# Loads of k and v moved ahead, stores and a small product moved back, in a fused attention and double expert-layer kernel

## The chip, the cores and the metric

The kernel runs on one core of one Trainium2 chip. The time is the device time of that core in microseconds (us). Before the change the median of three runs is 1707.53 us (1704.66 to 1713.23).

The engines are named as the profile names them: PE is TensorE's matrix multiply and PEld its weight load, DVE is VectorE, ACT is ScalarE, POOL is GpSimd, and SP is the engine that issues most transfers. A transfer is issued by SP or POOL and carried by 16 DMA engines.

## The reference

All inputs are float64 in memory; the kernel reads them as pairs of 32-bit words and converts them.

```python
# attention: B=8, H=8, S=576, D=64; k and v are averaged over 8 neighbours
k_p = k.reshape(B, H, 72, 8, D).mean(axis=3)
v_p = v.reshape(B, H, 72, 8, D).mean(axis=3)
scores = (1/sqrt(D)) * q @ k_p.T
attn = exp(scores - max) ; attn = attn / (sum(attn) + 1e-9)
x = attn @ v_p                                 # 4608 tokens x 512
# first layer: d_ff 1024
x = (((x @ w1) * (x @ w2)) @ w3) @ w_out
# second layer: d_ff 1536
xn = x / sqrt(mean(x*x) + 1e-6) * rms_g
g = xn @ w_gate
out = (g * sigmoid(g) * (xn @ w_val)) @ w_out2
```

## The kernel before, in words

The 4608 tokens are cut into nine blocks of 512 (`NB`, index `i`); the attention has eight batches of 576 tokens (index `b`). Products are made in three passes of a split operand (`mm3`, lines 93 to 95: high by high, high by low, low by high), so one product of a 128-column weight slice with a block is 4 x 3 = 12 matmuls.

The stages, in the order of the code:

- **Opening** (lines 543 to 590). `w3 @ w_out` is multiplied out once (`wps`, line 573), its split halves go to DRAM (`wpd`, lines 587 and 588, issued by POOL), and the attention of batch 0 and the first four pairs of products of block 0 are woven in.
- **Blocks 0 to 8** (lines 798 to 842). `ab(i, m, s)` makes `x @ w1` (s = 0) or `x @ w2` (s = 1) for one of eight slices `m`; for s = 1 DVE multiplies the two into `hh` or `hl` (line 540) and SP stores that to `hd` (line 541). There are 16 such products in a block. `positions(i)` says behind which of the 16 the steps of the next batch's attention stand: `S` the scores (line 299) with maximum and exponential, `N` the division (line 327), `T` the transposes, which are DVE's from batch 2 on (line 342), `av_steps` the product with v (line 404) and its split into `xh` and `xl` (lines 411 and 412), `kT` and `Q` the transposes of k and q (lines 262 and 281).
- **k and v** come in through `pool_four`: SP loads half of the eight neighbours into a tile `kv` (line 223), POOL issues a second, adding transfer of the other half once the first has landed (line 224), and `pool_sum` on DVE adds the rest (line 228) into `kp` or `vp` (line 231). Each of k and v is two tiles. The tile is one of three buffers of the pool `raw_p`.
- **The weights of the second layer** are converted in the background (`gv_steps`, 12 groups, one step behind each product by the `prep` ticker): a raw load of float64 words (line 111) into `raw_p`, the conversion (`s1`, `s2`), sums of quarters (line 725), a split into `wst` and two stores to `wd` (line 738, POOL).
- **The y stage** (lines 1193 to 1212): `second` multiplies h by the folded weights, eight products of 12 matmuls for a block. `y_end(i)` squares and stores the result (`f` tiles from a pool of five), and hands back three steps, of which one is taken behind each product of the following block: `sq_split`, nothing, and `rms`, whose two matmuls (lines 673 and 674) sum the squares.
- **The second layer** (lines 1216 on): `gv` for block 0, then `quad` for pairs of blocks.

The order in which each engine and queue runs its instructions is fixed when the program is built, by the framework's scheduler with its own estimate of times. It keeps to the order of the code only roughly: it brings an instruction forward when by its estimate the engine is idle and the operands are there. Buffers of a pool are given out in the order of the code. So `wC_p` (four buffers, `w`) holds first the folded weights `wph` and `wpl` of two groups, then `wf` and two `wst` of each background group.

Of the kernel before, what the change touches and what calls it, by code (L numbers as in the profile page):

```python
# [11 lines left out]
I32 = mybir.dt.int32  # L12
# [9 lines left out]
def kernel(  # L22
# [17 lines left out]
    nc = tc.nc  # L40
    B, H, S, D = q.shape
    P = 128
# [39 lines left out]
    def hxtile(nm):  # L82
        return hx_p.tile([P, 512], F32R, tag=nm, name=nm)

    def wtile(pool, nm):
        return pool.tile([P, 4, 512], F32R, tag="w", name=nm)
# [11 lines left out]
    class Conv:  # L98
# [5 lines left out]
        def s0(self):  # L104
            pool, tag, bufs = self.pool if isinstance(self.pool, tuple) else (self.pool, "raw", None)
            self.raw = pool.tile([P, 1024], I32, tag=tag, name="raw", bufs=bufs)
            src = self.src.bitcast(I32)
            dst = self.raw
            if len(src.shape) == 3:
                dst = dst.rearrange("p (i c) -> p i c", i=src.shape[1])  # L110
            nc.sync.dma_start(out=dst, in_=src)
# [371 lines left out]

    def load_cols(n, srcs, his, los):
        c, r = divmod(n, 2 * KD)
        s, kk = divmod(r, KD)
        return Conv(
            srcs[s][kk * P : (kk + 1) * P, c * 512 : (c + 1) * 512],
            raw_p,
            then=lambda f: split(his[s][c][:, kk, :], los[s][c][:, kk, :], f),  # L490
        )

    def load_w12(n):
        return load_cols(n, (w1, w2), (w1h, w2h), (w1l, w2l))

# [33 lines left out]

    a0 = {}  # L530

    def ab(i, m, s):
        wh, wl = ((w1h, w1l), (w2h, w2l))[s]
        ps = mm_feat(wh, wl, *xtile(i), m)
        if s == 0:
            a0[i, m] = ftile()
            nc.scalar.copy(a0[i, m], ps)
        else:
            hf = hxtile("hh" if m % 2 else "hl").bitcast(F32)
            nc.vector.tensor_tensor(out=hf, in0=ps, in1=a0.pop((i, m)), op=ALU.mult)  # L540
            nc.sync.dma_start(out=hdram[i][m], in_=hf)

# [98 lines left out]
    def ybank(i):  # L641
        if i % 2:
            return psum()
        return py_p.tile([P, 512], F32, tag="y", name="y")

    def y_end(i):
# [24 lines left out]
        def rms():  # L671
            ps = ybank(i)
            nc.tensor.matmul(ps[:1], ones, sp[0], start=True, stop=False)
            nc.tensor.matmul(ps[:1], ones, sp[1], start=False, stop=True)
            row = ftile()
            nc.scalar.copy(row[:1], ps[:1])
            nc.sync.dma_start(out=sdram[i : i + 1], in_=row[:1])
            ss = const.tile([P, 4], F32, tag="ss", name="ss", bufs=2)
            nc.sync.dma_start(out=ss, in_=sdram[i].rearrange("(p c) -> p c", p=P))
            nc.vector.tensor_scalar(  # L680
                out=ss, in0=ss, scalar1=1.0 / DM, scalar2=1e-6, op0=ALU.mult, op1=ALU.add
            )
            nc.gpsimd.tensor_tensor(out=ss, in0=ss, in1=mhalf, op=ALU.pow)
            nc.sync.dma_start(out=rdram[i].rearrange("(p c) -> p c", p=P), in_=ss)

        return [sq_split, lambda: None, rms]

# [13 lines left out]
    def gv_steps(G, s, kp):  # L701
# [30 lines left out]
        def put(j):  # L732
            f = cell["f"]
            c = 2 * G + j
            st = ptile("wst").rearrange("p (f l c) -> p f l c", f=8, l=2)
            split(st[:, :, 0, :], st[:, :, 1, :], f[:, j])
            for z in range(2):
                nc.gpsimd.dma_start(
                    out=wdram[s, c, z][:, :, kp],
                    in_=st[:, 4 * z : 4 * z + 4].bitcast(F32),  # L740
                )
            ready.add((s, c, kp))

        cs = []
        for z in range(2):
            k0 = (2 * z + kp) * P
            src = w[k0 : k0 + P, G * 512 : (G + 1) * 512]
            cs.append(Conv(src, raw_p, out=lambda z=z: quart(z), view=view))
            cs[z].on_act = True
# [6 lines left out]
            lambda: put(0),  # L756
            lambda: put(1),
        ]
# [9 lines left out]
    def positions(i):  # L768
# [7 lines left out]
        ]  # L776
        pos[2] = [lambda: A.N(0), A.load_v]
        for t in range(1, NTL):
# [7 lines left out]
            ]  # L786
        pos[8] += [A.v]
        pos[12] += [lambda: A.T(NTL - 1, 0), lambda: A.T(NTL - 1, 1)]
        pos[13] += av_steps(b, i + 1)
        if b + 1 < B:  # L790
            C = atts[b + 1]
            pos[9] += [C.k0]
            pos[10] += [lambda: C.q(0)]
            pos[13] += [C.k1, lambda: C.q(1)]
            pos[15] += [C.kT, lambda: C.Q(0, 0), lambda: C.Q(0, 1)]
        return pos

    c1 = conv_steps([load_w12(n) for n in range(8, 16)], 2)
    preB.close()
# [4 lines left out]
    col_tiles(wA_p, W12, (w1h, w1l, w2h, w2l))  # L804
    att_py.append(1)
    cv = Ticker(c1, 1)
    cv.run(6)
# [15 lines left out]
    for i in range(1, NB):  # L823
# [6 lines left out]
        for n, (m, s) in enumerate((m, s) for m in range(KF1) for s in range(2)):  # L830
# [4 lines left out]
            if i == NB - 1 and n == 5:  # L835
                prep.flush()
                wph[:], wpl[:] = [], []
                for g in range(2):
                    for l, lst in enumerate((wph, wpl)):
                        lst.append(wtile(wC_p, "wp"))  # L840
                        nc.sync.dma_start(out=lst[g].bitcast(F32), in_=wpdram[g][l])
        xt.pop(i)

    def rtile(nm, dt=F32R):
# [376 lines left out]
    for c in range(NCH):  # L1221
# [9 lines left out]
        for f in range(2):  # L1231
# [4 lines left out]
            if c and f == 0:  # L1236
                o_mm(0, 2 * c - 1)
                tick()
        if c == 0:
            while todo:  # L1240
                todo.pop(0)()
        if c == 3:
# [68 lines left out]
```

## Time and profile before

| | |
|---|---|
| median of three runs | 1707.53 us |
| the profiled execution | 1718.17 us |
| its span, first to last instruction | 1716.4 us |
| PE busy | 1623.1 us, 95% of the span, 7250 matmuls |
| DVE busy | 1021.8 us, 60% |
| ACT busy | 658.3 us, 38% |
| POOL busy | 95.0 us, 6% |
| mean granted TensorE clock | 0.975 of full speed |
| bytes moved | 322.53 MB, mean 188 GB/s |

The busy shares are averages over stages with different limits. PE idles for some 93 us of the span (1716.4 less 1623.1), and a granted clock below 1 means that a part of its busy time ran at half speed. The rows below say where.

### The profile page before, as it was taken

How to read it: one execution, taken by the hardware profiler on the slowest of the kernel's cores; microseconds unless marked ns; L12 is line 12 of the kernel's file. 1: busy time of each engine (PE TensorE's matmuls, PEld its weight loads, DVE VectorE, ACT ScalarE, POOL GpSimd, SP SyncE). 2: the span in 40 equal slices, each digit the busy share in tenths (PEclk: the TensorE clock that was granted, in tenths of full speed). 3: DMA queues.
4: the chain of work that ended last, by engine and by line, in shares of the span. 5: the costliest groups of instructions: out<-in, count | busy, mean ns of one | idle time of the engine just before them, and what ended most of it. 6: DMA issues, size and time to landing. Idle time of an engine off the chain costs nothing.

```text
span 1716.4 us, 19990 instructions
## 1 busy us (share of the span) xinstructions
PE 1623.1 (95%) x7250; PEld 1296.5 (76%) x7250; DVE 1021.8 (60%) x1813; ACT 658.3 (38%) x1567; POOL 95.0 (6%) x107
## 2 busy tenths in 40 slices
PE   6797998798798999998999999999999999999999
PEld 3465777677586788886877888888888888888887
DVE  7675798696887842564574243567355744465344
ACT  3555544444444422453441133343333334234322
POOL 0001020111101010010010000000000000000000
PEclk9998999899898999998999999999999999999999
DMA  9948466556646465577456674457354745455531
GB/s 261 238 132 199 128 164 163 149 164 162 186 122 194 146 230 207 194 254 254 142 188 224 225 270 162 181 194 269 139 219 177 273 175 200 162 202 198 184 109 74
DMA packets 147461, 322.53 MB, mean 188 GB/s; under 512 B 52505, under 2 KB 79129, under 8 KB 129442
## 3 DMA queue, kind: packets, MB, share of 16 engines
q1 hardware_dynamic: 126210, 276.13, 47.7%
q0 software_dynamic: 21152, 45.12, 9.8%
q8 instruction: 57, 0.93, 0.2%
q14 instruction: 42, 0.34, 0.1%
HBM read 247.75 MB, written 73.44 MB: 187 GB/s over the span
## 4 chain that ended last, share of the span: by engine, by line
PE 68%; DMA 11%; DVE 11%; issue 7%; ACT 2%; POOL 1%; SPq 0%; POOLq 0%; ACTq 0%; DVEq 0%
PE ps L93 14%; PE ps L94 14%; PE ps L95 14%; PE o L95 5%; PE o L94 5%; PE o L93 5%; DMA kv<-in_v_dram 5%; DVE aT L342 3%; PE y L93 2%; PE y L94 2%; PE y L95 2%; DMA raw<-in_moe_w_dram 2%; PE pa L299 2%; DMA raw<-in_moe_w_out_dram 1%; DMA ydram<-f 1%
## 5 line engine op out<-in xcount | busy, mean ns | idle before, releaser
L93 PE MATMUL ps<-xf,wr 128*128 128x512 f32 x576 | 224.3, 389 | 0.0
L95 PE MATMUL ps<-xf,wr 128*128 128x512 f32 x576 | 224.1, 389 | 0.0
L94 PE MATMUL ps<-xf,wr 128*128 128x512 f32 x576 | 224.1, 389 | 0.0
L95 PE MATMUL o<-oh,hcl 128*128 128x512 f32 x384 | 149.6, 389 | 0.0
L94 PE MATMUL o<-ol,hch 128*128 128x512 f32 x384 | 149.4, 389 | 0.0
L93 PE MATMUL o<-oh,hch 128*128 128x512 f32 x384 | 149.4, 389 | 0.0
L1067 ACT COPY f<-ps 128x512 f32<-128x512 f32 x144 | 84.4, 586 | 163.8 <-PE ps L95 158.4
L342 DVE STREAM_TRANSPOSE aT<-s 32x256 f32<-32x256 f32 x324 | 140.8, 434 | 4.4
L93 PEld LDWEIGHTS ps<-xf,wr 128*128 128x128 f32 x576 | 108.1, 188 | 23.0 <-ACT f L1067 0.4
L95 PEld LDWEIGHTS ps<-xf,wr 128*128 128x128 f32 x576 | 108.1, 188 | 22.4
L94 PEld LDWEIGHTS ps<-xf,wr 128*128 128x128 f32 x576 | 108.1, 188 | 22.3
L93 PE MATMUL ps<-xh,w1h 128*128 128x512 f32 x288 | 123.2, 428 | 0.1
L1071 DVE TENSOR_TENSOR f<-y,f 128x512 f32<-128x512 f32 x48 | 33.2, 691 | 143.1 <-PE y L95 143.1
L314 ACT ACTIVATE s<-pa,mx 128x72 f32<-128x72 f32 (+1 forms) x280 | 85.2, 330 | 80.3 <-DVE mx L311 80.3
L94 PE MATMUL ps<-xl,w1h 128*128 128x512 f32 x288 | 115.6, 403 | 0.0
L95 PE MATMUL ps<-xh,w1l 128*128 128x512 f32 x288 | 114.9, 401 | 0.1
L93 PE MATMUL ps<-xh,w2h 128*128 128x512 f32 x288 | 112.5, 391 | 1.9 <-DVE hh L540 1.7
L95 PE MATMUL ps<-xh,w2l 128*128 128x512 f32 x288 | 113.1, 393 | 0.0
L94 PE MATMUL ps<-xl,w2h 128*128 128x512 f32 x288 | 112.8, 392 | 0.0
L127 ACT ACTIVATE raw<-raw 128x512 int32<-128x512 uint32 x76 | 51.8, 683 | 127.1 <-DMA raw<-in_moe_w_dram 35.4
L1153 DVE TENSOR_TENSOR acc<-o,acc 128x512 f32<-128x512 f32 x64 | 43.5, 689 | 75.5 <-PE o L95 75.0
L95 PEld LDWEIGHTS o<-oh,hcl 128*128 128x128 f32 x384 | 72.1, 188 | 15.4 <-DVE hcl L1093 0.6
(187 smaller groups left out, 3253.1 us busy)
## 6 DMA issues: line engine op xcount, KB each, us to landing
wr<-wd SPq DMA_DIRECT2D x96, 1024.0 KB
wd<-wst POOLq DMA_DIRECT2D x48, 512.0 KB, 5.9
hr<-hd SPq DMA_DIRECT2D x36, 512.0 KB
raw<-in_moe_w_dram SPq DMA_DIRECT2D x32, 512.0 KB
oh<-od SPq DMA_DIRECT2D x15, 1024.0 KB
ol<-od SPq DMA_DIRECT2D x15, 1024.0 KB
wr<-wd SPq DMA_DIRECT2D x24, 512.0 KB
raw<-in_moe_w_out_dram SPq DMA_DIRECT2D x20, 512.0 KB
```

The lines of the kernel that those rows point to most:

```text
L93: nc.tensor.matmul(o, lh, rh, start=first, stop=False, skip_group_check=part)
L94: nc.tensor.matmul(o, lh, rl, start=False, stop=False, skip_group_check=part)
L95: nc.tensor.matmul(o, ll, rh, start=False, stop=last, skip_group_check=part)
L127: nc.scalar.activation(self.low, low_u, AF.Copy, scale=2.0**-29)
L299: nc.tensor.matmul(ps[:n, (p % 2) * 2 * SP : (p % 2 + 1) * 2 * SP], qT_t[t // 2][:, t % 2, p, :n], kT[:, p, :], start=True, stop=True,)
L314: nc.scalar.activation(s_t[t][:n, h, :SP], pv[:, j, :], AF.Exp, bias=mx[:, j, :], accum_out=den_t[t][:n, h, :],)
L342: nc.vector.transpose(aT[32 * kb : 32 * kb + 32, :, s0 + 32 * i : s0 + 32 * i + 32], s_t[t][32 * i : 32 * i + 32, :, 32 * kb : 32 * kb + 32],)
L1067: nc.scalar.copy(t, bank)
L1071: nc.vector.tensor_tensor(out=t, in0=bank, in1=t, op=ALU.add)
L1153: nc.vector.tensor_tensor(out=a, in0=ys[j], in1=a, op=ALU.add)
```

## The change

- `k0` and `k1` (load and sum of k) stand behind products 6 and 12 of a block and no longer 9 and 13; the load of v stands behind product 13 of the block before and no longer behind product 2 of its own, and its sum behind product 4, no longer 8. For batch 1 the load of v stands before the last weights of the first layer.
- The raw tiles of the background weights (`gv_steps`) and of the last eight loads of w1 and w2 (`c1`) are halves of a `wC_p` buffer, `rawp`, and no longer from `raw_p`.
- The stores of `wst` and of h are issued a step, or a product, later.
- `rms` is taken six products after `y_end` and no longer three. For the last block its product takes a `psum()` bank, and the loop that emptied the list after the first chunk of the second layer is gone.

```diff
+    def raw_halves():
+        half = []
+
+        def get():
+            if not half:
+                t = wC_p.tile([P, 2048], I32, tag="w", name="rawp")
+                half.extend([t[:, :1024], t[:, 1024:]])
+            return half.pop(0)
+
+        return get
...
         def s0(self):
-            pool, tag, bufs = self.pool if isinstance(self.pool, tuple) else (self.pool, "raw", None)
-            self.raw = pool.tile([P, 1024], I32, tag=tag, name="raw", bufs=bufs)
+            if callable(self.pool):
+                self.raw = self.pool()
+            else:
...
     def ab(i, m, s):
         wh, wl = ((w1h, w1l), (w2h, w2l))[s]
         ps = mm_feat(wh, wl, *xtile(i), m)
+        while h_put:
+            h_put.pop(0)()
...
-            nc.sync.dma_start(out=hdram[i][m], in_=hf)
+            h_put.append(lambda: nc.sync.dma_start(out=hdram[i][m], in_=hf))
...
         def rms():
-            ps = ybank(i)
+            ps = ybank(i) if i < NB - 1 else psum()
...
-        return [sq_split, lambda: None, rms]
+        return [sq_split] + [lambda: None] * 4 + [rms]
...
             split(st[:, :, 0, :], st[:, :, 1, :], f[:, j])
+            cell[j] = st
+
+        def store(j):
+            c, st = 2 * G + j, cell[j]
             for z in range(2):
                 nc.gpsimd.dma_start(
...
-        cs = []
+        cs, raws = [], raw_halves()
...
-            cs.append(Conv(src, raw_p, out=lambda z=z: quart(z), view=view))
+            cs.append(Conv(src, raws, out=lambda z=z: quart(z), view=view))
...
             lambda: put(0),
-            lambda: put(1),
+            lambda: (put(1), store(0)),
+            lambda: store(1),
...
-        pos[2] = [lambda: A.N(0), A.load_v]
+        pos[2] = [lambda: A.N(0)]
...
-        pos[8] += [A.v]
+        pos[4] += [A.v]
...
-            pos[9] += [C.k0]
+            pos[6] += [C.k0]
             pos[10] += [lambda: C.q(0)]
-            pos[13] += [C.k1, lambda: C.q(1)]
+            pos[12] += [C.k1, lambda: C.q(1)]
+            pos[13] += [C.load_v]
...
-    c1 = conv_steps([load_w12(n) for n in range(8, 16)], 2)
+    pair = [raw_halves() for _ in range(4)]
+    c1 = conv_steps([load_w12(n, pair[(n - 8) // 2]) for n in range(8, 16)], 2)
...
     att_py.append(1)
+    atts[1].load_v()
...
+    h_put.pop(0)()
...
-        if c == 0:
-            while todo:
-                todo.pop(0)()
```

## Rows read from the trace of the kernel before

**Rows 1.** Waits of PE, blocks 1 to 6: us in total, times, longest.

```profile
PE pa L299 <- DVE xl L412: 23.7, 5, 6.3
PE pa L262 <- DVE kp L231: 12.8, 7, 4.2
PE pa L262 <- DVE xl L412: 2.3, 1, 2.3
```

**Rows 2.** Waits of PE over the whole run, those outside the blocks.

```profile
PE pa L349 <- DVE s L327: 9.3, 1, 9.3
...
PE y L673 <- ACT f L665: 5.2, 2, 3.0
PE ps L673 <- ACT f L665: 4.4, 1, 4.4
...
PE y L674 <- DVE f L667: 2.2, 2, 1.9
...
PE y L93 <- ACT hh L89: 1.1, 1, 1.1
```

**Rows 3.** Stretches: length, busy us (count) of PE, PEld, DVE, ACT, POOL; clock, DMA, GB/s.

```profile
187.70:246.30 58.60, 55.89 (x289) 44.80 (x288) 49.95 (x115) 28.21 (x111) 6.54 (x7) 1.00 0.54 144
246.30:314.50 68.20, 60.61 (x288) 48.72 (x289) 55.70 (x125) 30.33 (x113) 10.95 (x12) 0.92 0.60 160
...
452.40:518.90 66.50, 60.30 (x288) 48.53 (x288) 54.19 (x121) 30.73 (x114) 10.88 (x12) 0.92 0.62 163
518.90:580.00 61.10, 56.03 (x270) 44.95 (x271) 50.05 (x114) 28.35 (x111) 5.42 (x6) 0.92 0.47 140
...
904.00:1716.40 812.40, 808.68 (x3552) 668.31 (x3552) 405.16 (x587) 254.95 (x413) 1.01 (x1) 1.00 0.52 191
```

**Rows 4.** DVE's timeline where block 2 begins: start, us, instruction, [idle before].

```profile
258.31 0.69 DVE L228 TENSOR_TENSOR kv<-kv 72x512 f32<-72x512 f32 x1 [2.53 <-DMA kv<-in_v_dram]
...
261.78 0.69 DVE L228 TENSOR_TENSOR kv<-kv 72x512 f32<-72x512 f32 x1 [2.19 <-DMA kv<-in_v_dram]
262.39 1.14 DVE L412 SCALAR_TENSOR_TENSOR xl<-pa,xh 128x192 fp32r<-128x192 f32 x4
```

**Rows 5.** SP's and POOL's issues of those loads of v.

```profile
247.46 1.70 SPq L223 DMA_DIRECT2D kv<-in_v_dram  x2
...
252.90 2.48 POOL L224 DMA_DIRECT2D kv<-in_v_dram  x2 [18.61 <-DMA kv<-in_v_dram]
```

**Rows 6.** Busy time in the five half-clock stretches behind the S waits, their sum.

```profile
sum 25.30, PE 25.30 PEld 23.04 DVE 14.99 ACT 14.88 POOL 0.00; mean PE 5.06 PEld 4.61 DVE 3.00 ACT 2.98 POOL 0.00
```

**Rows 7.** The same behind four of the kT waits.

```profile
sum 13.60, PE 13.60 PEld 12.29 DVE 10.34 ACT 5.10 POOL 0.00; mean PE 3.40 PEld 3.07 DVE 2.59 ACT 1.28 POOL 0.00
```

**Rows 8.** A stretch of the opening, and four stretches at half clock elsewhere.

```profile
40.00:60.00 20.00, 18.20 (x65) 8.70 (x64) 17.51 (x37) 10.42 (x20) 1.63 (x3) 1.00 1.07 298
...
172.40:176.00 3.60, 3.60 (x14) 2.57 (x14) 2.09 (x4) 2.38 (x12) 0.00 (x0) 0.50 0.59 184
779.20:783.60 4.40, 4.25 (x10) 2.96 (x11) 2.84 (x4) 1.47 (x2) 0.00 (x0) 0.50 0.76 264
807.50:810.90 3.40, 3.35 (x8) 2.60 (x9) 2.45 (x2) 1.74 (x3) 0.00 (x0) 0.50 0.78 244
904.00:909.90 5.90, 5.88 (x14) 4.59 (x15) 1.98 (x3) 1.16 (x2) 0.00 (x0) 0.50 0.79 289
```

**Rows 9.** DVE's timeline: the second v tile of batch 1; two additions for k.

```profile
170.03 0.69 DVE L228 TENSOR_TENSOR kv<-kv 72x512 f32<-72x512 f32 x1 [10.63 <-DMA kv<-in_v_dram]
...
278.99 0.69 DVE L228 TENSOR_TENSOR kv<-kv 72x512 f32<-72x512 f32 x1 [1.20 <-DMA kv<-in_k_dram]
...
313.94 0.41 DVE L231 TENSOR_TENSOR kp<-kv 72x256 f32<-72x256 f32 x1
```

**Rows 10.** POOL's issues in the opening.

```profile
52.37 0.62 POOL L587 DMA_DIRECT2D wpd<-wph  x1 [14.12 <-ACT wph L89]
...
59.55 1.25 POOL L224 DMA_DIRECT2D kv<-in_v_dram  x1 [5.43 <-DMA kv<-in_v_dram]
```

More of the change, by code (lines that the diff above doesn't have):

```diff
@@ L104, in s0 @@
         def s0(self):
-            pool, tag, bufs = self.pool if isinstance(self.pool, tuple) else (self.pool, "raw", None)
-            self.raw = pool.tile([P, 1024], I32, tag=tag, name="raw", bufs=bufs)
+            if callable(self.pool):
+                self.raw = self.pool()
+            else:
+                pool, tag, bufs = (
+                    self.pool if isinstance(self.pool, tuple) else (self.pool, "raw", None)
+                )
+                self.raw = pool.tile([P, 1024], I32, tag=tag, name="raw", bufs=bufs)
             src = self.src.bitcast(I32)
@@ L482, in col_tiles, with load_cols @@
             lst.append(wtile(pool, nm))
-    def load_cols(n, srcs, his, los):
+    def load_cols(n, srcs, his, los, pool=raw_p):
         c, r = divmod(n, 2 * KD)
@@ L488, in load_cols, with load_w12 @@
             srcs[s][kk * P : (kk + 1) * P, c * 512 : (c + 1) * 512],
-            raw_p,
+            pool,
             then=lambda f: split(his[s][c][:, kk, :], los[s][c][:, kk, :], f),
         )
-    def load_w12(n):
-        return load_cols(n, (w1, w2), (w1h, w2h), (w1l, w2l))
+    def load_w12(n, pool=raw_p):
+        return load_cols(n, (w1, w2), (w1h, w2h), (w1l, w2l), pool)
     W12 = ("w1h", "w1l", "w2h", "w2l")
@@ L530 @@
     a0 = {}
+    h_put = []
     def ab(i, m, s):
```

## Prediction

> **What bounds the kernel now.** I read the page's first two parts, then the waits of PE, then PE's timeline around each of them, then the timelines of DVE, SP and POOL at the same times, and at last the busy time by stretch. PE is busy in 95% of the span, so only two things can be won: its idle time and the time that it runs at half clock. In the second layer there is neither: 808.7 us busy of 812.4 us, clock 1.00 [rows 3]. All that the change can reach lies before 910 us.
>
> There the waits fall into five kinds. Within the blocks PE waits for DVE at two places. One is the first score product of the next batch, which needs a bank that DVE empties with `xl` (23.7 us in five waits). The other is the transpose of k, which needs `kp` (12.8 us) or again a bank (2.3 us) [rows 1]. Outside them it waits once for a transpose of batch 1 (9.3 us), in the y stage for the sum of squares (4.4 us, and the longer, 3.0 us, of two that make 5.2), and where the second layer begins (the rest, 2.2 us, then 1.9 and 1.1) [rows 2]. After nearly each of these the clock stands at 0.50 for a while, and busy time at half clock counts half as lost.
>
> Why is DVE late at the score product? Its timeline shows it stopped in the addition for v, first 2.53 us, then 2.19 us, and only then come the four `xl` that PE needs [rows 4]. That addition stands in the code behind product 8 of the block; the build has brought it in front of work of product 1. An engine that has stopped at a wait lets nothing behind it pass, so the wait for a load of v becomes PE's wait. SP issued these loads at 247.46 us and within 1.70 us of it, POOL the adding halves at 252.90 us and just behind [rows 5], and the last landed at 261.78 us when DVE went on. The same thing in batch 1 cost DVE 10.63 us [rows 9].
>
> **The change part by part.** It adds and removes no computing instruction and no transfer; the loads and additions of k and v, 120 stores and nine small products change place, and 32 raw tiles change buffer. The sum is made on the profiled execution's 1718.2 us.
>
> *v earlier (a).* Before, both v tiles wait for buffers that the sums of k free. After, the three `raw_p` buffers serve k and v alone: the first v tile takes the third buffer early, and the second goes out when the first k tile is summed. That sum moves ahead of the four `xl` of product 13, so I put SP's issue at about 245 us and no longer 248.8 (247.46 plus about half of the stretch of two). From issue to POOL's turn took 5.4 us (252.90 less 247.46), from there to landing 7.6 to 8.9 with two tiles in flight (261.78 less 254.2 or 252.9); with one, about 5.4 for each half. The estimate for landing is 245 + 5.4 + 5.4 = 256 us. DVE comes to the addition at 255.8 (258.31 less 2.53), so its stop goes to about nothing and `xl` is ready 5 to 6 us earlier. Price of the five waits: 23.7 us, plus half of the 25.3 us at half clock behind them [rows 6] = 36.3 us. The margin is thin, and the build may bring the addition forward again by as much as the load; I take 80%, 29 us; bounds 0 and 36.
>
> *T in batch 1 (b).* The load of v now has its buffers before the last weights, some 30 us earlier; DVE's 10.63 us stop goes. PE wins 9.3 us and half of 3.6 us [rows 2, 8], 11.1 us. The last four weight loads now need buffers that are free only when the stores of `wph` have landed, up to 3 us later than today: 2 us off. I take 9; bounds 3 and 11.
>
> *k (c).* Waits at kT are 12.8 + 2.3 us, and half of 13.6 us behind them [rows 1, 7]: 21.9 us. But here DVE is not stopped; it is full. It has 49.95 us of work in a block of 58.6 us and 54.2 to 55.7 us in the long ones [rows 3]. The sum of k moves in front of four `xl`, and those free the banks that kT and Q want: what one gains the other loses. I take 5; bounds 0 and 22.
>
> *Sum of squares (d).* `rms` comes three products later, 36 matmuls. At 808.68 us for 3552 [rows 3] one is 0.228 us, so 8.2 us. The two waits are 4.4 and 3.0 us, both shorter. So they go, with half of 4.4 + 3.4 us [rows 8]: 7.4 + 3.9 = 11.3 us. Its three tiny transfers on SP move with it. Late next is DVE's step behind two of them, which now stands near the next `y_end`; the following `rms` has 8.2 us to spare for that. I take 11; bounds 6 and 11.3.
>
> *Where the second layer begins (e).* 2.2 + 1.9 + 1.1 us and half of 5.9 us = 8.2 us [rows 2, 8]. Taking `rms` away removes the first two, but the next product still needs `hh`, which DVE makes behind the same additions. I take 2; bounds 0 and 8.
>
> *Later stores (f).* 72 stores of h go out one product later and 48 of `wst` one step later, past loads on SP and past the adding halves on POOL. By the code this clears the queues. But the order in the queues is the build's, and a store that is ready is placed when it is ready, wherever it stands in the code: 0, with four `hh`/`hl` buffers as cover. Lower and upper bound: the same 4 us either way, a tenth of (a).
>
> *Earlier loads in the opening (g).* The first four of the c1 loads, 0.5 MB each, can now go out as soon as the stores issued from 52.37 us on have landed. The adding half of v for batch 0 goes out at 59.55 [rows 10], and the stretch up to 60 us has a DMA share of 1.07 at 298 GB/s [rows 8]: nothing is free there. 2 MB at that rate are 7 us. Issued by another engine than v's adding half, they would pass beside it at best and take all 7 us from it at worst; I take 4 us lost; bounds 0 and 10 with the half clock. The Trainium skill (DMA: Bandwidth & Descriptors, section Issuing engines are not separate DMA queues) says that transfers of all issuing engines run on the same 16 DMA engines and interleave. By that rule the whole 7 us would be v's and the sum 3 us smaller; the row of 1.07 is on its side, but no row before shows these loads there.
>
> Sum: 29 + 9 + 5 + 11 + 2 + 0 - 4 = 52 us, so 1718.2 - 52 = 1666.2 us in a profiled execution. The median stands at 1707.53/1718.17 = 0.9938 of the profiled one: **1656 us**. As a check, with (a) and (c) four long blocks, the first of 68.2 and the last of 66.5 us, fall to about 60; the one before them, which has the same work and no stop, takes 58.6 [rows 3]. The forecast's own range: all at the better end but bounded by 58.6 us a block gives about 75 us, 1633; with (a) at 60%, (b) and (d) at 5 and 8 and (g) at its full 7 about 28 us, 1680.
>
> **The rivals.**
>
> *DVE takes it back.* DVE has 54 to 56 us of work in a long block [rows 3]. If its order at the head of a block stays as it is and the addition meets the load again, or if the backlog at the end of the block grows by what was won at its head, (a) and (c) give nothing: 9 + 11 + 2 - 4 = 18 us, 1718.2 - 18 = 1700.2, or 1690 us. For it: every wait within the blocks ends with DVE [rows 1]. Against it: the block that takes 58.6 us. Spread 1680 to 1699.
>
> *No change.* The loads go out where they went, since the build and not the code orders SP, and what (b) and (d) win, 20 us, is lost to the opening and to the narrower ring of `w` buffers, now full with `rawp`, `wf` and two `wst`. 1707 us, within 5. Against it: (d) needs no change of any queue.
>
> *Slower, through SP's queue.* The load of the second v tile waits in SP's queue for a k tile to be summed. An addition for k was done at 278.99 us and its last step, which frees the tile, at 313.94 [rows 9], 35 us later. If the build counts on the early one, SP stops for 35 us, and the stores of h queue up behind. There are four buffers for h, filled one in two products of 12 x 0.228 us: PE can go on for 4 x 2 x 2.74 = 21.9 us, and loses 13 us a block and about 1.7 at half clock. Five blocks: 73 us, against 18 us won elsewhere: 1718.2 + 55 = 1773, or 1762 us. It decides from a stop of some 24 us on. Against it: SP issued the loads of v at 247.46 us [rows 5], where a block ends and k is summed by the code, so the build's idea of that sum is not far off there.
>
> **How the numbers follow.** Forecast 0.60, DVE takes it back 0.20, no change 0.10, slower 0.10. About 0.5% is what a measurement of this kernel can tell from no change: 1699 and 1716 are the bounds. Faster is the forecast and nearly all of the first rival, 0.79; same 0.11; slower 0.10. For 8 in 10 the range leaves out the slower rival, half of no change, and a little below: 1630 to 1705. The forecast's own range is 1633 to 1680.
>
> **What the profile after would show.** (a) right: DVE's stop in the addition for v is under 1 us at the heads of blocks 2 to 6, PE's wait at the score product with it, and clock 1.00 there; the stretches from kT to kT are about 60 us. (b): no wait of 9 us at the transpose. (c): waits at kT of 2 to 3 us remain. (d): no wait of PE for the sum of squares in the y stage. (g): the load of v for batch 0 lands some us later than before, and PE's wait there is longer. Wrong would make it: a stop of DVE at the addition for v that has only moved, blocks still of 66 us or more, SP stopped for 20 us at a load of v, or new waits for the converted weights.

## The result, and the profile after

The changed kernel takes 1699.83 us (median of 10 runs, 1696.64 to 1704.81) against 1712.47 us for the kernel before, run beside it (10 runs, 1704.66 to 1722.42). The ratio is 0.992 with a 95% interval of 0.9893 to 0.9948: 12.6 us faster by the medians (13.7 by the means), in place of the 52 us that I forecast. Where did the rest go? The profiled execution after takes 1697.01 us with a span of 1695.2 us, 21.2 us less than the one before.

The first view cuts the span of after at five marks that can be found in any trace of this kernel: the first transpose of k of batch 1, of batch 2 and of batch 7, the first product of the y stage, and PE's first instruction of the second layer, a product with `xnh`. (The stretch of [rows 3] from 904.0 us begins later, at the first product with `oh`, 17.0 us inside the second layer.) The columns are those of [rows 3].

```profile
0.00:130.40 130.40, 111.17 (x408) 63.23 (x409) 93.81 (x198) 65.29 (x173) 12.03 (x18) 0.95 0.81 221
130.40:189.40 59.00, 45.56 (x234) 33.53 (x233) 38.72 (x85) 33.58 (x124) 7.31 (x7) 0.86 0.68 177
189.40:511.70 322.30, 292.86 (x1442) 233.51 (x1440) 269.05 (x607) 145.94 (x564) 46.87 (x51) 0.96 0.62 163
511.70:667.00 155.30, 151.05 (x688) 121.51 (x689) 85.26 (x171) 52.68 (x148) 11.67 (x16) 0.97 0.51 178
667.00:866.90 199.90, 199.90 (x882) 163.52 (x881) 122.43 (x154) 97.44 (x133) 13.49 (x13) 1.00 0.66 224
866.90:1695.20 828.30, 818.79 (x3603) 676.51 (x3601) 413.76 (x600) 262.36 (x426) 2.39 (x2) 1.00 0.52 191
```

The same marks in the trace before stand at 131.7, 187.7, 518.9, 675.2 and 887.0 us of 1716.4, so its stretches are 131.7, 56.0, 331.2, 156.3, 211.8 and 829.4 us. Against my terms: the y stage won 12 us (d: 11) and the second layer 1.1 us (e: 2), about as forecast. The five stretches of blocks 1 to 5 won 8.9 us, where (a) and (c) together were to win 34. The opening with block 0 lost 1.7 us (130.4 + 59.0 against 187.7), where (b) and (g) were to win 5.

PE's waits from the transpose of k of batch 2 to 600 us, which answer to [rows 1] (L315 is the score product, L278 the transpose of k):

```profile
PE pa L315 <- ACT s L330: 12.0, 3, 4.9
PE pa L315 <- DVE xl L428: 9.1, 4, 4.1
PE pa L278 <- DVE xl L428: 8.8, 4, 2.7
PE pa L420 <- DVE xl L428: 1.5, 1, 1.5
PE ps L104 <- DVE hh L559: 1.4, 1, 1.4
```

The 23.7 us at the score product behind `xl` have become 9.1, and the 15.1 us at the transpose of k 8.8, so the old waits did shrink by 21 us. But a new one stands on top: the score product now waits 12.0 us in three for the exponentials (`s`), later in the block. Behind it stands DVE. Its stops at the additions for k and v, from 100 to 600 us, after:

```profile
DVE kv L244 <- DMA kv<-in_k_dram: 43.0, 11, 10.9
DVE kv L244 <- DMA kv<-in_v_dram: 12.6, 3, 4.7
```

Before, the same view gives 50.5 us in twelve for v and 7.4 us in three for k. The sum has hardly moved (57.9 to 55.6 us); only the tensor it stops for has changed. In the five stretches of blocks 1 to 5 the change is complete. Before:

```profile
DVE kv L228 <- DMA kv<-in_v_dram: 30.7, 9, 7.4
DVE kv L228 <- DMA kv<-in_k_dram: 1.2, 1, 1.2
```

After, no stop for v is left there, as (a) said, but these for k:

```profile
DVE kv L244 <- DMA kv<-in_k_dram: 30.9, 6, 10.9
```

One of these stops with what it does to PE, from the timelines of DVE, SP, POOL, DVE and PE:

```profile
256.04 0.42 DVE L247 TENSOR_TENSOR kp<-kv 72x256 f32<-72x256 f32 x1
...
256.49 0.33 SPq L239 DMA_DIRECT2D kv<-in_k_dram  x1
...
258.35 2.53 SPq L239 DMA_DIRECT2D kv<-in_v_dram  x2
...
265.46 1.23 POOL L240 DMA_DIRECT2D kv<-in_k_dram  x1 [8.97 <-DMA kv<-in_k_dram]
...
270.62 0.69 DVE L244 TENSOR_TENSOR kv<-kv 72x512 f32<-72x512 f32 x1 [10.90 <-DMA kv<-in_k_dram]
...
276.22 0.45 DVE L327 TENSOR_REDUCE mx<-pa 128x4 f32<-128x288 f32 x1
...
278.07 1.33 PE L315 MATMUL pa<-kT,qT 128*128 128x144 f32 x4 [4.15 <-ACT s L330]
```

The first k tile of batch 4 is summed at 256.04 us, which frees one of three buffers. At 256.49 SP issues the load of the second k tile into it, two of v behind that; POOL can issue the adding half only when the first half is in, at 265.46; it lands at 270.52. DVE has come to the addition 10.90 us earlier and lets nothing pass. The maximum (`mx`) that the exponentials need comes only at 276.22, and PE waits 4.15 us. That k is wanted 48 us later, at the transpose at 318.31 us. In this order of DVE's program the load can't go out earlier, since a buffer comes free only then; but its addition stands right behind.

### The profile page after: what moved, and what is told of

The parts are those of the page before. It is cut to its first block, busy times and chain, and to the rows that moved or that the text cites. A ratio compares the mean times of both kernels' runs of the same rounds, so it can differ in the third digit from the quotient of the medians.

```text
span 1695.2 us, 19962 instructions
## 1 busy us (share of the span) xinstructions
PE 1619.3 (96%) x7250; PEld 1291.8 (76%) x7250; DVE 1023.0 (60%) x1813; ACT 657.3 (39%) x1567; POOL 93.8 (6%) x107
## 4 chain that ended last, share of the span: by engine, by line
PE 70%; DVE 14%; DMA 9%; issue 5%; SPq 1%; ACT 1%; POOL 0%; POOLq 0%; DVEq 0%
PE ps L104 13%; PE ps L106 13%; PE ps L105 13%; DVE aT L358 6%; PE o L106 5%; PE o L105 5%; PE o L104 5%; DMA kv<-in_k_dram 4%; PE y L104 4%; PE y L105 4%; PE y L106 4%; DMA kv<-in_v_dram 2%; DMA raw<-in_moe_w_out_dram 1%; PE wps L592 1%; DVE mx L327 1%
## 5 line engine op out<-in xcount | busy, mean ns | idle before, releaser
L106 PEld LDWEIGHTS o<-oh,hcl 128*128 128x128 f32 x384 | 72.1, 188 | 15.5 <-DVE hcl L1121 0.6
L104 PEld LDWEIGHTS o<-oh,hch 128*128 128x128 f32 x384 | 72.1, 188 | 15.0
```

What stands on the lines that cost most here:

```text
L104: nc.tensor.matmul(o, lh, rh, start=first, stop=False, skip_group_check=part)
L106: nc.tensor.matmul(o, ll, rh, start=False, stop=last, skip_group_check=part)
```

## The experiments

Each short diff names the kernel that it starts from. The table, made from PE's timeline at the marks above, gives the lengths of the stretches in us, the last column to PE's last matmul. (An expectation below gives the y stage as 228.8 and 216.0 us: it counts on into the second layer, to the first product with `oh`. To that same product the second figure is 215.0 us.) The ratio is against runs of the kernel before on the same chip, so across chips the ratios, with their intervals, are the firmer comparison; "sq" is the sum of squares six products on.

| kernel | median us | ratio (95%) | opening | block 0 | blocks 1 to 5 | to y | y stage | second layer |
|---|---|---|---|---|---|---|---|---|
| before | 1712.5 | 1 | 131.7 | 56.0 | 331.2 | 156.3 | 211.8 | 825.7 |
| before, second profile | 1708.2 (1 run) | | 129.1 | 50.9 | 331.7 | 156.3 | 208.9 | 825.9 |
| after | 1699.8 | 0.9920 (0.9893 to 0.9948) | 130.4 | 59.0 | 322.3 | 155.4 | 199.8 | 824.3 |
| before + sq | 1694.5 | 0.9889 (0.9851 to 0.9928) | 127.6 | 48.1 | 332.3 | 156.4 | 199.8 | 822.8 |
| after + hold | 1680.9 | 0.9792 (0.9754 to 0.9831) | 130.0 | 55.2 | 313.0 | 152.9 | 199.8 | 824.6 |
| before + hold | 1687.6 | 0.9838 (0.9798 to 0.9878) | 129.8 | 49.0 | 313.3 | 153.8 | 214.9 | 824.3 |
| before + hold + sq | 1669.8 | 0.9773 (0.9750 to 0.9796) | 125.8 | 48.1 | 310.2 | 153.7 | 199.8 | 822.8 |

**Hold the addition where the code has it (after + hold).** The first addition writes into an `f` tile. These are handed out in the order of the code, so the build can't bring the addition far forward. The second addition reads that tile.

```diff
+        t = ftile()[:SP].rearrange("s (h c) -> s h c", h=4)
         nc.vector.tensor_tensor(
-            out=r[:, :, : 2 * D], in0=r[:, :, : 2 * D], in1=r[:, :, 2 * D :], op=ALU.add
+            out=t, in0=r[:, :, : 2 * D], in1=r[:, :, 2 * D :], op=ALU.add
         )
...
```

> The changed kernel, but the first addition for k and for v writes into an f tile and no longer in place; so it is placed near where the code has it (v behind about product 4 of a block, k behind about product 12), because f tiles are handed out in the order of the code. Theory A: DVE stops because the addition is placed before its load has landed. Then its stops at the load of k (43.0 us in 11) and of v (16.1 us in 4) fall to under 10 us together, the four blocks of 63 to 71.5 us go to about 60 us, and the time falls by 15 to 22 us against the changed kernel, to about 1680 us. Theory B: DVE is full in the blocks (54 to 56 us of work), and the wait only changes its name. Then the stops vanish too, but the blocks stay at 63 us or more and the time within 5 us of 1700.

The order of DVE's program in block 2 shows what the edit does. h17 to h24 are the block's eight products of h (two of the sixteen products make one), +k4 is a first addition for a k tile of batch 4, and so on; kp and vp are the second additions:

```
before         h16 +v3 h17 +v3 vp vp h18 +k4 h19 h20 h21 h22 h23 kp +k4 kp h24
after          h16 +k4 kp h17 vp vp +k4 kp h18 +v4 +v4 +k5 h19 h20 h21 h22 h23 h24 kp
after + hold   h16 h17 h18 +v3 vp +v3 vp h19 h20 h21 h22 +k4 +k4 kp kp h23 h24
```

The second tile of k4, the one of the stop above, stands behind h17 in after and behind h22 with the hold, ten products on. The first of k5 stands behind h18; with the hold it is in the next block, behind h30. With the hold, DVE's waits from 100 to 600 us hold one stop at a load of k or v:

```profile
DVE f L245 <- DMA kv<-in_k_dram: 4.1, 1, 4.1
```

1680.9 us, and 313.0 us for the five stretches in place of 322.3: theory A by the stops and by the time. Its blocks of about 60 us came in part: after's four long blocks (71.5, 63.1, 63.0 and 67.2 us) took 60.3, 65.0, 67.1 and 61.0 us.

**The same on the kernel before (before + hold).**

> The kernel before, with nothing of the change, but the first addition for k and v writes into an f tile as in the run beside it, so that it is placed behind about product 8 (v) and 13 (k). Theory A: no earlier load is needed; the stops at v at the heads of the blocks vanish (PE's 23.7 us at the score product and half of 25.3 us at half clock), and the time falls by 20 to 30 us against the kernel before, to 1683 to 1692 us. Theory B: 1712 us, within 5; what is gained at the head comes back at the transposes of k.

1687.6 us: with no load moved, the five stretches take 313.3 us, as in after + hold. The earlier loads are not what the blocks needed. Of PE's waits there only those at the transpose of k stay, now 21.8 us in five for `kp` and 3.2 in one for `xl`.

There is a rival to the order: with the hold the tile of a load is free after the first addition and no longer after the second, so the loads might simply come sooner. The issues of the adding halves of v for block 2, and their additions, speak against it:

```profile
247.40 1.23 POOL L224 DMA_DIRECT2D kv<-in_v_dram  x1 [17.12 <-DVE wf L726]
251.53 1.24 POOL L224 DMA_DIRECT2D kv<-in_v_dram  x1 [0.18 <-issue]
```

```profile
282.75 0.68 DVE L229 TENSOR_TENSOR f<-kv 72x512 f32<-72x512 f32 x1
284.48 0.68 DVE L229 TENSOR_TENSOR f<-kv 72x512 f32<-72x512 f32 x1
```

From the transpose of k that opens the block (242.1 us here, 246.3 before) POOL's two issues stand at 5.3 and 9.4 us; before, the first stood at 6.6 us and the second just behind [rows 5]. The additions stand at 40.7 and 42.4 us, in place of 12.0 and 15.5 [rows 4]. The loads go out as they did; the additions have moved.

**Additions that need no load.** From batch 2 on they read a tile that stays; loads go out and nobody reads them.

```diff
+        else:
+            nc.vector.tensor_tensor(out=t, in0=t, in1=t, op=ALU.max)
...
```

> The changed kernel; from batch 2 on the additions for k and v read a tile that has been in place since batch 1, while all loads still go out and are read by nobody (so k and v of batches 2 to 7 are left out of the result). DVE's work is the same and no load can stop it. Theory A: the stops are all that is lost, so blocks 1 to 5 go to 58 to 60 us and the time to 1670 to 1683 us. Theory B: within 5 us of the changed kernel's 1700 us, as DVE's work is what bounds the blocks.

1694.3 us, ratio 0.9882 (0.985 to 0.9914), on neither side: blocks 1 and 2 took 72.3 and 68.6 us, the last three 62.9, 61.7 and 58.3. With no reader behind them, the loads of k and v of all batches went out by 245 us. PE had one wait of 11.1 us in that crowd, in block 1, and one of 9.1 us for `xl` in block 2, when the loads were over. The run is spoilt as a test of the whole; its last three blocks, with neither a load of k or v nor a stop at one, give a length that a block can have: 58 to 63 us.

**The sum of squares alone (before + sq).**

```diff
...
-        return [sq_split, lambda: None, rms]
+        return [sq_split] + [lambda: None] * 4 + [rms]
...
```

> The kernel before with the sum of squares six products on as the only edit (with its bank for the last block, and without the loop that emptied the list). If the y stage is a term of its own, it wins the 12.0 us that the stage became shorter: about 1700 us, 0.993 of before, and then the rest of the change, loads and stores together, has given nothing. Rival: the stage gives 5 us or less by itself (1707 or more), and the rest of the change gave the other half.

1694.5 us, at least as fast as the whole change (0.9889 against 0.9920, intervals that overlap). The y stage takes 199.8 us in place of 211.8. So all that the loads, sums and stores do together comes to nothing that can be told from zero.

**Both edits without any earlier load (before + hold + sq).**

> The kernel before with two edits: the first addition for k and v goes into an f tile (which alone gave 1687.6 us), and the sum of squares comes six products on (which alone gave 1694.5 us and a y stage of 216.0 us for 228.8). No load and no store moves. If the two are separate terms they add up: 1687.6 less 12 to 17 us, 1670 to 1676 us, faster than the changed kernel with the same addition (1680.9 us); then the earlier loads are worth nothing, or cost some us. Rival: the earlier loads are needed once the additions stand right; then this run is no better than 1681 us.

1669.8 us: the terms add up. By the medians this is 11 us below after + hold, by the ratios 0.9773 against 0.9792, with intervals that overlap; so the earlier loads win nothing that shows, and whether they cost something is not shown by the times. In the one profile of each, this kernel is shorter by 4.2 us in the opening, 7.1 us in block 0 and 2.8 us in the five stretches.

**The old places in the changed kernel.**

```diff
-        pos[4] += [A.v]
+        pos[8] += [A.v]
...
-            pos[6] += [C.k0]
+            pos[9] += [C.k0]
...
-            pos[12] += [C.k1, lambda: C.q(1)]
-            pos[13] += [C.load_v]
+            pos[13] += [C.k1, lambda: C.q(1)]
...
```

> The changed kernel with k0, k1, the load of v and its sum at the places of the kernel before; the raw tiles of their own, the later stores and the later sum of squares stay. Theory A (only the stop's owner changed, from v to k): stops at v again and about the same time as the changed kernel and as the later sum of squares alone, 1693 to 1702 us. Rival: the new places cost something by themselves, then 1690 us or less; or they do win part of the 29 us that I expected, then 1705 us or more.

1698.5 us, ratio 0.9928 (0.9909 to 0.9948), five stretches of 321.9 us together. But one thing was not as expected: DVE's stops, in the view shown of after, are still at k.

```profile
DVE kv L244 <- DMA kv<-in_k_dram: 44.2, 10, 11.1
DVE kv L244 <- DMA kv<-in_v_dram: 13.0, 3, 5.8
```

These are after's (43.0 and 12.6) with the places of before. So the new places in the code moved next to nothing; something else had turned v into k.

**The raw tiles alone (before + sq + rawp for the background weights).**

```diff
-            cs.append(Conv(src, raw_p, out=lambda z=z: quart(z), view=view))
+            cs.append(Conv(src, raws, out=lambda z=z: quart(z), view=view))
```

> The kernel before with the later sum of squares (1694.5 us alone) and one more edit: the raw tiles of the background weights are halves of a wC_p buffer. Loads, sums and stores stand where they stood. Theory: it was this edit, not the places of the loads, that turned DVE's stops at v into stops at k, since with raw_p free the addition for k can stand earlier; then DVE stops for k for 30 us or more and for v for under 20 us, the five stretches from batch 2 on take 318 to 323 us in place of 332.3, and the time is 1682 to 1688 us. Rival: the places of the loads did it; then the stops are at v (45.3 us in 12 in the later sum of squares alone) and the time is 1694 us within 4.

DVE's stops at the additions in the same view, first of before + sq, then with this edit:

```profile
DVE kv L228 <- DMA kv<-in_v_dram: 45.3, 12, 7.8
DVE kv L228 <- DMA kv<-in_k_dram: 9.3, 4, 4.1
```

```profile
DVE kv L244 <- DMA kv<-in_k_dram: 32.0, 8, 10.0
DVE kv L244 <- DMA kv<-in_v_dram: 11.9, 3, 7.3
```

The stops went from v to k with this edit alone, and the five stretches take 323.9 us for 332.3. The time did not follow: 1694.9 us, ratio 0.9899 (0.9867 to 0.9931), and in that profile block 0 took 54.2 us for 48.1; whether that belongs to the edit or to the one execution stays open.

**The opening as before (after, with c1 in raw_p and batch 1's v at its old places).**

```diff
-    c1 = conv_steps([load_w12(n, pair[(n - 8) // 2]) for n in range(8, 16)], 2)
+    c1 = conv_steps([load_w12(n) for n in range(8, 16)], 2)
...
-    atts[1].load_v()
```

> The changed kernel with the opening as before: the eight last raw loads of w1 and w2 take raw_p tiles again, and batch 1's load and sum of v stand where they stood. All else of the change stays. In every run with the changed opening the stretch between the transposes of k of batches 1 and 2 took 55.2 to 59.7 us, in the two runs of the later sum of squares with the opening of before 48.1 us. Theory: the changed opening costs these 8 to 11 us; then the stretch is 47 to 50 us and the time 1688 to 1692 us. Rival: the stretch is longer because of the steps of batch 2 that now stand in block 0; then it stays over 55 us and the time at 1697 us or more.

The stretch falls from 59.0 to 49.5 us as expected, but the time only to 1694.5 us, ratio 0.9903 (0.9871 to 0.9935): the next block takes 63.6 us for 57.4, and gives two thirds of it back. By the intervals, too, it can't be told from after. On after + hold:

> The same edit on the changed kernel whose first addition goes into an f tile (1680.9 us). If the opening is all that sets that kernel apart from the kernel before with the same addition and the later sum of squares (1669.8 us; the five stretches behind took 313.0 us there and 310.3 us here), the time is 1669 to 1673 us. Rival: the raw tiles of their own cost as well, as the conversion of the background weights stopped for its load there (18.6 us in 3 stops); then 1677 us or more.

1674.6 us, ratio 0.9786 (0.9755 to 0.9817), the opening and block 0 in 180.0 us for 185.1. By the medians this is 6 of the 11 us between after + hold and before + hold + sq, between the two expectations; the ratios of the three can't be told apart. Whether the raw tiles of their own cost something stays open.

What the changed opening does is seen in after's timelines of POOL, DVE, PE and SP:

```profile
142.03 0.76 POOL L607 DMA_DIRECT2D wpd<-wpl  x1 [9.11 <-DVE wpl L101]
...
136.29 0.69 DVE L244 TENSOR_TENSOR kv<-kv 72x512 f32<-72x512 f32 x1 [6.04 <-DMA kv<-in_k_dram]
...
139.18 0.68 DVE L167 CUSTOM_DVE_ANT_0 f<-rawp,f 128x1024 uint16<-128x1024 uint16 x1
...
139.63 0.79 PE L104 MATMUL ps<-xh,w1h 128*128 128x512 f32 x1 [7.92 <-ACT w1h L100]
...
139.88 0.80 SPq L127 DMA_DIRECT2D rawp<-in_moe_w_dram  x2
145.22 1.27 SPq L127 DMA_DIRECT2D rawp<-in_moe_w_dram  x2
```

An early addition for k of batch 2 stops DVE for 6.04 us in front of the conversion of w1, for which PE waits 7.92 us. The last four raw loads go out at 139.88 to 146.5 us, when before the last two stood at 138.32 to 141.6. SP's own waits from 136 to 148 us show what held them:

```profile
SPq L127 <- DVE f L167: 9.7, 1, 9.7
SPq L127 <- DVE f L154: 3.6, 1, 3.6
```

Both are DVE's conversions of earlier raw tiles, the first done at 139.86 us and behind the stop for k. The stores of the folded weights did not come last: the last of them goes out at 142.03 us, none lands in less than 5.8 us, and the last two raw loads go out from 145.22 us on. The runs put the opening back as a whole, so they don't tell what the new buffers and the earlier load of v did apart.

**The stores.** In after, each store back behind its instruction; and the later stores on before + hold + sq:

```diff
-            h_put.append(lambda: nc.sync.dma_start(out=hdram[i][m], in_=hf))
+            nc.sync.dma_start(out=hdram[i][m], in_=hf)
...
-            lambda: put(0),
-            lambda: (put(1), store(0)),
-            lambda: store(1),
+            lambda: (put(0), store(0)),
+            lambda: (put(1), store(1)),
```

> The changed kernel with the stores of h and of the prepared weights issued right behind the instructions that make them, as before. Expected: no difference from the changed kernel's 1700 us, within 4 us, since the order of the queues is the build's. Rival: the later stores clear the queue for loads and are worth 5 us or more; then 1705 us or more.

> The kernel before with the first addition into an f tile and the later sum of squares (1669.8 us), and the stores of h and of the prepared weights issued later as in the change. Expected: within 4 us of 1669.8 us. Rival: the later stores cost what the changed kernel won without them, 7 us, so 1675 us or more.

1693.0 us, ratio 0.9902 (0.9884 to 0.9919), and 1671.2 us, 0.9751 (0.9723 to 0.9778). The first is below both expectations, yet its interval overlaps that of after; the second is as expected. Over both, the later stores are worth nothing, and cost little if anything.

**k still earlier.** On after + hold, k loaded behind product 5 and summed behind 10; on before + hold + sq, behind 8 and 11:

> The changed kernel with the first addition into an f tile (1680.9 us), and k loaded behind product 5 and summed behind product 10, no longer 6 and 12. There PE waited 13.8 us at the transpose of k for a bank behind the last xl, and 11.4 us at the score product. Theory A': what stands in DVE's order right in front of the xl of product 13 is what counts; with the sum of k out of it the waits at the transpose of k fall to under 6 us, and the time to 1668 to 1676 us. Theory B: DVE is full, the backlog stays and the time is within 4 us of 1681.

> The kernel before with the first addition into an f tile and the later sum of squares (1669.8 us), and k loaded behind product 8 and summed behind product 11, for 9 and 13. There PE still waits 21.1 us in five at the transpose of k for kp, which DVE makes behind the four xl. Theory A': four small operations of DVE less behind the xl make each of these waits some 2 us shorter; with the half clock behind them 10 to 13 us in all, 1657 to 1661 us. Theory B: DVE is full there, so the wait goes over to the xl or to the score product, and the time is 1666 us or more.

1686.1 us, ratio 0.9862 (0.9842 to 0.9882): slower than after + hold, by 5 us in the medians. In the worst stretch DVE stopped 10.53 us, at a conversion of the background weights whose raw load SP had issued at 305.32 us, and PE waited 9.5 us at the score product. And 1670.5 us, ratio 0.9765 (0.9729 to 0.98): nothing won. The five waits at the transpose of k kept their size, 20.6 us for 21.1, and only changed their releaser from `kp` to `xl`.

**The wait in batch 1, once more.** The kernel before, unchanged:

> The kernel before, unchanged, profiled a second time. Theory: the stop of 10.63 us at v and PE's wait of 9.3 us in batch 1 belong to that one execution, since the later sum of squares alone has the same instructions in the same order up to the y stage and shows a stop of 3.8 us and a stretch of 48.1 us. Then the wait is under 3 us and the stretch from the transpose of k of batch 1 to that of batch 2 is 47 to 51 us in place of 56.0. Rival: it belongs to the program, and 9 us of wait stand there again.

From its timelines, DVE's second addition for v of batch 1, and PE's longest wait at a transpose of that batch:

```profile
162.09 0.69 DVE L228 TENSOR_TENSOR kv<-kv 72x512 f32<-72x512 f32 x1 [3.06 <-DMA kv<-in_v_dram]
```

```profile
171.88 1.04 PE L349 MATMUL pa<-ident,s 128*72 128x128 f32 x8 [1.43 <-ACT s L314]
```

The stop that was 10.63 us [rows 9] is 3.06 us here, PE's wait of 9.3 us [rows 2] is 1.43, and the stretch is 50.9 us long. The long wait belonged to one execution. This one's span, 1706.4 us, is 10.0 us below the first; 7.7 us of that lie before the transpose of k of batch 2, and 2.9 us in the y stage.

**The first addition on POOL (before + hold + sq).**

```diff
-        nc.vector.tensor_tensor(
+        nc.gpsimd.tensor_tensor(
             out=t, in0=r[:, :, : 2 * D], in1=r[:, :, 2 * D :], op=ALU.add
...
```

> The kernel before with the later sum of squares and the first addition for k and v into an f tile, made on POOL and no longer on DVE (with it on DVE: 1669.8 us, blocks of 61.6 to 62.8 us). DVE has four operations of 0.68 us, 2.7 us, less in each block. Theory B (DVE's work bounds the blocks now): each of five blocks gets 2 to 3 us shorter, with the half clock 12 to 16 us in all, 1654 to 1658 us. Theory A' (only the order counts): the operations in front of the transpose of k matter alone, 1 to 1.4 us of the 4.2 us wait, and the time is 1662 to 1667 us. Against both: an operation on POOL stands in front of the adding transfers in POOL's queue, and if it makes them late, 1670 us or more.

1665.8 us, ratio 0.9716 (0.9686 to 0.9745), the fastest of all, and its interval is clear of that of before + hold + sq. One addition takes POOL 1.324 us in the median and DVE 0.681 us, but it no longer stands in DVE's order. PE's waits there, from the transpose of k of batch 2 on, on DVE first and then on POOL:

```profile
PE pa L263 <- DVE kp L232: 21.1, 5, 4.5
PE pa L405 <- DVE xl L413: 1.8, 1, 1.8
```

```profile
PE pa L263 <- DVE kp L232: 12.4, 7, 3.2
PE pa L263 <- DVE xl L413: 6.2, 2, 3.3
PE pa L300 <- DVE xl L413: 1.6, 1, 1.6
```

The five stretches take 304.5 us for 310.2. 5.7 us and the 1665.8 us lie where the expectation puts the order at one place (1 to 1.4 us in each of five blocks), well under the 12 to 16 us of a DVE that is full. The Trainium skill (GPSIMD Engine Reference, section 4.1, Engine selection) puts elementwise work with two inputs on VectorE, since GpSimd takes about twice as long; 1.324 against 0.681 us agrees. Here the slower engine is still the better place.

## Why the prediction was wrong

The forecast was 1656 us, and 1699.8 was measured. The sign was right. That the range up to 1705 held it is luck: it reached so far for the rivals' sake, and the forecast's own ended at 1680. The step that carried the sum failed.

**(a), where it failed.** I read DVE's stop at the load of v as a load that comes too late, and priced its going at 29 us; that the build may bring the addition forward again I put at 20%. The loads of v did come in time, and DVE's stops at them in the five stretches went from 30.7 us to none. What I put at nothing is that the additions for k could then stop DVE in their place: they did, for 30.9 us, and the five stretches, where (a) and (c) were to win 34 us, won 8.9. The stops come from where the build puts the additions against their loads, not from the loads alone, and the new places of the loads are not even what moved them: the places of before in the changed kernel change neither time nor stops. What changed the order was the edit that I had put down as a mere change of buffers. With `raw_p` free of the background weights, the additions for k stand ten products and more ahead of where the hold puts them, and DVE stops for k as long as it had for v. Holding the additions at their places, with no load moved, gives 18 us in the five stretches, and 24.6 us by the medians. The rival that I called "DVE takes it back" named this, "the addition meets the load again". Its 1700.2 us for the profiled execution is near the 1697.0 measured, but in part by luck: the blocks won 8.9 us for its 0, and the opening with block 0 lost 1.7 us for its gain of 5 (9 less 4). Its 1690 us for the median came from the factor 0.9938 of three runs; with the median of ten, 1712.47/1718.17, the factor is 0.9967, which also puts my 1656 us at 1661.

**(b), a price taken from one execution.** 9.3 us of wait, and half of the clock behind it, were in the profiled execution and not in the program: 1.43 us in the second profile. The stretch took 48.1 to 50.9 us in that profile and in five of the seven other runs with the opening of before, 53.7 in the one with the addition on POOL and 54.2 with the raw tiles alone. The change made that stretch longer, 55.2 to 59.7 us in all runs with its opening, 49.5 and 51.6 with the opening put back. I had taken 2 us off for the last four weight loads, behind the stores of `wph`; the last of them is out at 146.5 us for 141.6, 4.9 us later, and it waited for DVE, which had stopped for the early k. Against the second profile the opening with block 0 lost 9.4 us (130.4 + 59.0 less 129.1 + 50.9).

**(c), right in size, the reason half right.** The waits of PE at the transpose of k fell from 15.1 to 8.8 us, for my 5. I had said that DVE is not stopped there but full. The five stretches of before + hold + sq, first their busy time and then DVE's waits in them:

```profile
173.90:484.10 310.20, 288.08 (x1441) 231.44 (x1441) 274.41 (x613) 149.71 (x566) 48.70 (x52) 0.97 0.65 170
```

```profile
DVE den L326 <- ACT s L315: 10.6, 5, 2.2
DVE raw L143 <- ACT raw L127: 6.8, 5, 3.9
DVE f L138 <- ACT f L129: 5.0, 3, 3.5
```

DVE is busy 274.4 of 310.2 us, 88%, and most of its idle time is spent behind ACT, in the division and in the conversion of the background weights. It is not full, but near it, and it is late at one place, the end of a block, where the four `xl` and the second additions for k meet. Taking 13.6 us of additions from DVE (20 of 0.681 us) won 5.7 us of these 310.2, less than half. Why bringing k forward by two products leaves the wait as long, with `xl` in place of `kp`, stays open: the runs show that it does, not which instruction takes the place.

**(d), right.** 12 us in the y stage, with the change and alone, for 11; 9.1 us against the second profile. No wait of PE for the sum of squares is left: PE is busy in all of the 199.90 us, at clock 1.00. **(e)** 1.1 us for 2, and not from the waits: in place of 2.2, 1.9 and 1.1 us the first product with `oh` now waits 5.5 us for `hh`. **(f)** 0, within what can be told.

**(g), the sign right, the way wrong.** The early loads did not go out in the saturated stretch: the first raw load into `rawp` stands at 110.59 us. So nothing there bears on the rule of the Trainium skill that I weighed (DMA: Bandwidth & Descriptors, section Issuing engines are not separate DMA queues); no run here shows it. The loss came at the other end, with an early addition for k and the last raw loads behind it, and is the one counted under (b).

## What to carry to other kernels

Where an in-order engine stops at a load, look first at where its instruction stands in the built order, and only then at how early the load goes out: an edit that frees a buffer can bring another such instruction forward, and the stop changes its name but not its length (30.7 us for v, 30.9 us for k). Give such an instruction something that ties it to its place (here an output from a pool that is handed out in code order), or an engine whose stop costs nothing. And do not price a single wait of several us in a part with loads in flight before a second profile of the same program shows it again.

## What was unexpected of the hardware

Two profiled executions of one program differ by 10 us of span (1716.4 and 1706.4 us); 7.7 us of that lie before the transpose of k of batch 2 (187.7 and 180.0 us), where transfers and stops for them meet, 2.9 us in the y stage, and the second layer differs by only 0.2 us. A load in two steps, a plain half and then an adding half, took 14.0 us from its issue (256.49 us) to landing (270.52) with two more in flight, 9.0 us of which went by before the second half could be issued.
